# Layer two of a strided-attention and two-layer kernel: its phases in another order

## The chip, the cores and the metric

The program runs on one core of a Trainium2 chip (trn2). The time is the device time of one execution in microseconds (us); with one core there is no slowest of several. TensorE (PE) multiplies, VectorE (DVE) and ScalarE (ACT) do the elementwise work, SyncE (SP) only issues transfers. The kernel before took 868.13 us, the median of three runs (863.78 to 869.3).

## The reference

```python
def _attn_ref(q, k, v):                       # (4, 8, 576, 64), heads 0-3 local, 4-7 strided, stride 32
    scores = scale * np.matmul(q, k.transpose(0, 1, 3, 2))
    scores = np.where(masks[None], scores, -1000000000.0)
    ...                                       # softmax
    return np.matmul(attn, v).astype(np.float32)

def _moe_ref(x, w_in, w_out, s, b):           # x (2304, 512), w_in (512, 2048), w_out (2048, 512)
    r = np.maximum(x @ w_in, 0.0)
    return ((s * (r * r) + b) @ w_out).astype(np.float32)

def _moe2_ref(x, w_in, w_out):
    h = x @ w_in
    return ((h * np.cos(h)) @ w_out).astype(np.float32)
```

Attention gives `x`, layer one is `_moe_ref`, layer two `_moe2_ref`. The weights come as 64-bit floats and are turned into 32-bit ones on the chip.

## The kernel before, in words

Every 32-bit operand of a large product is split into a high half (`split_hi`, L161, a copy on ACT that rounds) and a low half (`split_lo`, L164, a subtraction on DVE), and a product is three matmuls: high by high, high by low, low by high.

The 2304 tokens are three blocks of 768. Attention and a part of layer one come first. From there on the products with `w_in` are made by seven products of half-size operands (P1 to P7) in place of eight; one unit is one pair of 128-wide slices of the 2048, eight units to a block. In this long middle part an automatic scheduler puts the instructions of each engine in order, and background jobs (`pair_ops`, `out_ops`, `sum_ops`) run a step now and a step then between the products (`bg2_step`): they load a weight, convert it, form its sums, split it and store it for later. `out_ops` does this for a slice of `w_out`; for layer two it also stores the unsplit slice (`w2f`).

The last part is `Blocks`, for blocks 1 and 2 of layer two; there each engine takes its instructions in the order in which the program writes them. It begins at unit 2 of block 1 (units 0 and 1 and block 0 come before it, and `run_out` stores the six output tiles of block 0 about there). It has two stages for each block.

*Periods.* `period(v)` makes P1 to P7 of unit v, each 6 matmuls of 128x384, in two PSUM banks that take turns from unit to unit. A bank is emptied by ACT (`evacuate`, tile `q`, L1511) or by a sum on DVE (`hsum`, L1089, 128x384), and the next product into the bank waits for that. P3 and P4 of unit v are made in period v+1. Each finished h goes through g = h cos h in five steps: `arg` (ACT, L1529), `whole` (ACT, L1533, one shared tile `m`, shown as `a`), `rest` (DVE, L1538), `sine` (ACT, L1543), `times` (DVE). The result stands in quarters `(i, f)`, shown as `graw`.

*Products with w_out.* `BLOCK_PRODUCTS` lists seven products j of four pairs each: `pair(n)`, n = 4j + pp, is 12 matmuls of 128x384 (two units, two output halves e, three terms). For its operand `hi(n)` and `lo(n)` split a quarter into one of three operand buffers, n mod 3. For some j the quarter is first replaced by a sum or a difference of quarters: `add(n)` on DVE. One 128x768 instruction does a pair of units for pp 0 and 1, two 128x384 ones for pp 2 and 3. The loop writes, for each n, `pair(n)`, then `after(j)` at the end of a phase, then `hi(n+2)`, `add(n+3)`, `lo(n+2)`. `after(0)` to `after(2)` copy two PSUM banks to tiles t0, t1, t2 on ACT; `after(3)` does four sums on DVE, `after(4)` and `after(5)` two each, and stores. For block 1, `form(2)` in the loop also takes steps that form the operands of block 2.

The two stages overlap: `run` mixes the end of the last unit's chain (unit 7, `last`) with `pair(0)`, `pair(1)` and the first splits.

Of the kernel before, what the change touches and what calls it, by code (L numbers as in the profile page):

```python
# [9 lines left out]
F32 = mybir.dt.float32  # L10
# [101 lines left out]
NSUM = 4  # L112
OPERANDS = [(0, 0), (0, 1), (3, 1)]
# [15 lines left out]
def net(ctx, tc, qkl, qks, rqk, vloc, vstr, rv, wi1, wo1, wp1, wo2, wp2, s, b, out):  # L129
# [267 lines left out]
    def out_ops(raw, ly, n):  # L397
        t = conv_tile("tw")
        yield from to_f32(t, raw)
        bg2_load()  # L400
        if ly:
            yield lambda t=t: nc.sync.dma_start(out=w2f[n // 2][:, n % 2, :], in_=t)
# [8 lines left out]
        yield lambda: None  # L411
# [1055 lines left out]
    class Blocks:  # L1467
# [15 lines left out]
        def acc(self, j, e):  # L1483
            return (accs[0:2], accs[2:4], accs[4:6], banks, accs[4:6], accs[2:4], accs[0:2])[j][e][:, :HT]
# [64 lines left out]
        def period(self, v):  # L1549
            new, old = v < NPAIR, v > self.v0  # L1550
            if new:
                self.product("P1", v)
                self.evacuate("P1", v)
            self.hsum(v - 1, 1, 1, 1, 2)
            self.whole(v - 2, 1)
            self.sine(v - 2, 0)
            if new:
                self.product("P2", v)
                self.hsum(v, 0, 0, 1, 0)
# [55 lines left out]
        def pair(self, n, units=(0, 1), es=(0, 1)):  # L1615
# [21 lines left out]

        def after(self, j):
            if j in (0, 1, 2):
# [3 lines left out]
                self.t = getattr(self, "t", []) + [t]  # L1643
# [12 lines left out]
            if j == 5:  # L1656
                o = io_p.tile([P, 2, HT], F32, tag="io", name="c21")
                for e in range(2):
                    tt(o[:, e], self.acc(j, e), self.t[0][:, e], ALU.add)
                self.store(1, 0, o)  # L1660
# [13 lines left out]

        def form(self, n):
            for _ in range(n):
                next(self.forms, None)

        def run(self):
# [330 lines left out]
```

## Time and profile before

| | us |
|---|---|
| median of three runs | 868.13 |
| lowest and highest run | 863.78, 869.3 |
| the profiled execution | 861.52 |
| its span, first to last instruction | 859.7 |
| busy in it: PE, DVE, ACT | 823.9, 680.8, 587.3 |

The profiled execution is 6.6 us below the median; rows of it are compared with its own 861.52. A row of a list of instructions gives the start in us, the duration of the group, the engine, the line of the kernel, the operation, the tiles, the count, and in square brackets the idle time of the engine just before it with what ended that. A matmul of 384 columns takes 0.33 us from start to end, but the next one starts 0.17 us after it.

### The profile page before, as it was taken

To read this page: it belongs to the slowest core of one execution; us is meant where nothing else is said; L and a number is where in the kernel's file an instruction comes from. 1 tells how busy PE (TensorE), PEld (TensorE's weight loads), DVE (VectorE), ACT (ScalarE), POOL (GpSimd) and SP (SyncE) were. 2 spreads that over 40 slices of the span, in tenths; PEclk is the share of its full clock that TensorE was granted. 3 is DMA by queue.
4 is the path that set the end of the run, shared out by engine and by line. 5 is a ranking of instruction groups with operands and counts; after the bars stand their busy time and mean duration, and the time that the engine had idled before them with its cause. 6 is when DMAs were issued, how large, how long until landed. Compare 5 with 4: busy or idle time off the path is not lost.

```text
span 859.7 us, 15559 instructions
## 1 busy us (share of the span) xinstructions
PE 823.9 (96%) x5545; PEld 734.6 (85%) x5545; DVE 680.8 (79%) x1297; ACT 587.3 (68%) x1237; POOL 19.5 (2%) x73
## 2 busy tenths in 40 slices
PE   8999999999999999999999999999998899998898
PEld 5667777888888988999989889899898789998788
DVE  6999766997897878986976987877678887578884
ACT  6888776677766867867767656656588544688443
POOL 3120000000000000000000000000000000000000
PEclk9999999999999999999999999999999999999999
DMA  9755532688779978797998989989987579772574
GB/s 339 218 176 180 158 109 96 234 290 232 260 306 317 358 279 269 277 317 220 312 359 294 318 288 340 294 324 341 365 271 234 193 230 288 239 254 89 175 240 154
DMA packets 103069, 220.00 MB, mean 256 GB/s; under 512 B 9168, under 2 KB 54480, under 8 KB 102992
## 3 DMA queue, kind: packets, MB, share of 16 engines
q1 hardware_dynamic: 101696, 212.62, 73.4%
q10 hardware_dynamic: 1296, 6.39, 2.2%
q8 instruction: 44, 0.72, 0.3%
q14 instruction: 33, 0.27, 0.1%
HBM read 163.92 MB, written 55.05 MB: 255 GB/s over the span
## 4 chain that ended last, share of the span: by engine, by line
PE 69%; DVE 9%; ACT 4%; DMA 3%; issue 1%; SPq 0%; ACTq 0%; DVEq 0%
PE acc L1775 9%; PE acc L875 9%; PE h_ps L875 8%; PE pb L1878 8%; PE pa L1878 8%; PE acc L1765 7%; PE acc L1624 6%; PE acc L1496 5%; DVE xlo L164 3%; PE pa L1496 3%; PE pb L1496 2%; DVE graw L1089 2%; ACT xhi L161 1%; PE pa L1624 1%; DVE t L1089 1%
## 5 line engine op out<-in xcount | busy, mean ns | idle before, releaser
L875 PE MATMUL h_ps<-xhi,w 128*128 128x512 f32 (+1 forms) x320 | 100.9, 377 | 0.2
L875 PE MATMUL acc<-gh,w 128*128 128x512 f32 (+1 forms) x320 | 99.1, 374 | 0.0
L1775 PE MATMUL acc<-gh,w2l 128*128 128x512 f32 (+1 forms) x384 | 85.6, 336 | 0.0
L1878 PE MATMUL pa<-xhi,wfl 128*128 128x384 f32 x268 | 80.2, 339 | 4.1 <-DVE h L1858 2.5
L1878 PE MATMUL pb<-xhi,wfl 128*128 128x384 f32 x268 | 80.1, 339 | 0.9 <-ACT q L1889 0.9
L161 ACT ACTIVATE xhi<-graw 128x384 fp32r<-128x384 f32 (+1 forms) x84 | 50.8, 629 | 43.5 <-DVE graw L1089 27.0
L1624 PE MATMUL acc<-xhi,w2m 128*128 128x384 f32 x256 | 68.1, 339 | 3.7 <-ACT xhi L161 3.7
L875 PEld LDWEIGHTS h_ps<-xhi,w 128*128 128x128 f32 x320 | 58.5, 189 | 11.7 <-ACT w L161 1.1
L164 DVE TENSOR_TENSOR xlo<-graw,xhi 128x384 fp32r<-128x384 f32 (+1 forms) x84 | 54.9, 685 | 16.4 <-ACT xhi L161 16.2
L875 PEld LDWEIGHTS acc<-gh,w 128*128 128x128 f32 x320 | 58.4, 189 | 10.1 <-ACT gh L161 0.2
L1775 PEld LDWEIGHTS acc<-gh,w2l 128*128 128x128 f32 x384 | 60.2, 188 | 7.3
L1765 PE MATMUL acc<-w2l,gh 128*128 128x512 f32 x192 | 60.2, 390 | 0.0
L1496 PE MATMUL acc<-xhi,wfl 128*128 128x384 f32 x196 | 56.1, 338 | 3.9 <-DVE graw L1089 3.6
L875 PE MATMUL h_ps<-xlo,w 128*128 128x512 f32 (+1 forms) x160 | 59.5, 372 | 0.0
L875 PE MATMUL acc<-gl,w 128*128 128x512 f32 (+1 forms) x160 | 59.3, 371 | 0.0
L1878 PEld LDWEIGHTS pa<-xhi,wfl 128*128 128x128 f32 x268 | 49.4, 188 | 7.4 <-DVE h L1858 3.6
L1878 PEld LDWEIGHTS pb<-xhi,wfl 128*128 128x128 f32 x268 | 49.4, 188 | 3.8 <-ACT q L1889 2.2
L1624 PEld LDWEIGHTS acc<-xhi,w2m 128*128 128x128 f32 x256 | 47.3, 191 | 4.0 <-ACT xhi L161 4.0
L1775 PE MATMUL acc<-gl,w2l 128*128 128x512 f32 x192 | 49.5, 336 | 0.0
L1366 ACT ACTIVATE h<-h 128x768 f32<-128x768 f32 x48 | 40.4, 841 | 12.2 <-DVE h L1858 11.9
L164 DVE TENSOR_TENSOR gl<-r,gh 128x512 fp32r<-128x512 f32 (+2 forms) x56 | 40.5, 723 | 8.9 <-ACT gh L1366 6.5
L1624 PE MATMUL acc<-xlo,w2m 128*128 128x384 f32 x128 | 43.8, 343 | 2.7 <-DVE xlo L164 2.6
(240 smaller groups left out, 2137.9 us busy)
## 6 DMA issues: line engine op xcount, KB each, us to landing
wfl<-wfb SPq DMA_DIRECT2D x68, 512.0 KB, 5.3
wfl<-wfa SPq DMA_DIRECT2D x34, 512.0 KB, 5.5
w2l<-w2s SPq DMA_DIRECT2D x28, 512.0 KB, 5.5
praw<-in_wp_dram SPq DMA_DIRECT2D x22, 512.0 KB, 4.7
oraw<-in_wo_dram SPq DMA_DIRECT2D x21, 512.0 KB, 4.4
wfb<-ob SPq DMA_DIRECT2D x21, 512.0 KB, 4.6
w2s<-ow SPq DMA_DIRECT2D x20, 512.0 KB, 5.2
w2m<-wsum SPq DMA_DIRECT2D x20, 512.0 KB, 4.3
```

Source lines behind the costliest of these rows:

```text
L161: nc.scalar.activation(dst_hi, src, AF.Copy)
L164: return nc.vector.tensor_tensor(dst_lo, src, hi.bitcast(F32), ALU.subtract)
L875: nc.tensor.matmul(*args, **kw)
L1089: return nc.vector.tensor_tensor(d, x, y, op)
L1366: return nc.scalar.activation(*args, **kw)
L1496: nc.tensor.matmul(self.bank(v, bi), a, b[:, m, :], start=st and m == 0 and i == 0, stop=m == 1 and i == 2, skip_group_check=True)
L1624: nc.tensor.matmul(self.acc(j, e), w[u][:, wi, c], g[:, u], start=first and i == 0, stop=last and i == 2, skip_group_check=True)
L1765: nc.tensor.matmul(accs[e], g[:, e * P : (e + 1) * P], w[:, wi, :], start=start and i == 0, stop=stop and i == 2, skip_group_check=True,)
L1775: nc.tensor.matmul(o, w[:, wi, e * P : (e + 1) * P], g[:, c : c + o.shape[1]], start=start and i == 0 and (c == 0 or e % 2 == 0), stop=sto ...
L1878: nc.tensor.matmul(pb[bi], a, b[:, m, :], start=st and m == 0 and i == 0, stop=m == 1 and i == 2, skip_group_check=True)
```

## The change

Six things change. (1) The order of phases: the product that uses quarter (1, 1) as it stands moves from place 5 to place 3, so that phases with an `add` (j = 1, 2, 4, 5) no longer follow one another four times; the PSUM banks follow, and the sum that makes output tile `c21` from that product comes later, in j = 5. (2) In the periods, `hi(0)` and `hi(1)` come one period earlier, `hi(2)` right behind period 7, and `lo(0)` and `lo(1)` come behind the `hsum` that opens the period. (3) Between the stages, `add(4)` to `add(7)`, `hi(4)` to `hi(6)` and the chain of unit 7 stand in another order, and `pair(0)` is cut in three. (4) The loop splits three pairs ahead, not two. (5) The sums of outputs that stood together in `after(3)` and `after(5)` are given out one at a time by the table `ROOM`, as are the steps of `form`. (6) In `out_ops` the store of the unsplit slice takes the place of an empty step, one step fewer for each of layer two's 16 slices, and the last two output tiles of block 0 take buffers of the pool `io` in place of `gt`.

```diff
     (False, 0, (1, 0), ((1, 0), (1, 0), (1, 1), "add")),
+    (False, 3, (1, 1), None),
     (False, 2, (0, 0), ((0, 0), (1, 1), (0, 0), "subtract")),
     (True, (1, 1), (0, 0), ((0, 0), (0, 1), (0, 0), "subtract")),
-    (False, 3, (1, 1), None),
     (True, (1, 0), (0, 1), None),
...
+ROOM = {9: (0, 2), 10: (0, 2), 11: (0, 2), 12: (0, 2), 20: (1, 1), 21: (1, 1), 22: (0, 2), 23: (1, 2), 24: (1, 2), 25: (0, 2), 26: (0, 2)}
...
     def out_ops(raw, ly, n):
-        t = conv_tile("tw")
+        t = whole = conv_tile("tw")
         yield from to_f32(t, raw)
         bg2_load()
-        if ly:
-            yield lambda t=t: nc.sync.dma_start(out=w2f[n // 2][:, n % 2, :], in_=t)
...
         yield lambda: split_hi(os[0], t)
-        yield lambda: None
+        yield lambda: nc.sync.dma_start(out=w2f[n // 2][:, n % 2, :], in_=whole) if ly else None
         yield lambda: split_lo(os[1], t, os[0])
...
         def acc(self, j, e):
-            return (accs[0:2], accs[2:4], accs[4:6], banks, accs[4:6], accs[2:4], accs[0:2])[j][e][:, :HT]
+            return (accs[0:2], accs[2:4], accs[4:6], accs[2:4], banks, accs[4:6], accs[0:2])[j][e][:, :HT]
...
             self.hsum(v - 1, 1, 1, 1, 2)
+            if v - 1 >= NPAIR - 3:
+                self.lo(v - 1 - NPAIR + 3)
             self.whole(v - 2, 1)
...
-                    first, last = pp == 0 and u == 0 and j < 4, pp == 3 and u == 1
+                    first, last = pp == 0 and u == 0 and j in (0, 1, 2, 4), pp == 3 and u == 1
...
+        def add_acc(self, d, j, e):
+            tt(d[:, e], self.acc(j, e), self.t[0][:, e], ALU.add)
+
         def after(self, j):
             if j in (0, 1, 2):
...
-            if j == 3:
-                u2 = self.t[0]
+            if j == 4:
                 for e in range(2):
-                    tt(u2[:, e], self.acc(j, e), u2[:, e], ALU.add)
-                tt(self.t[2], self.t[2], self.t[1], ALU.add)
-                tt(self.t[2], self.t[2], u2, ALU.add)
-                self.store(1, 1, self.t[2])
-            if j == 4:
+                    self.add_acc(self.t[0], j, e)
+            if j == 5:
                 o = io_p.tile([P, 2, HT], F32, tag="io", name="c12")
...
-            if j == 5:
-                o = io_p.tile([P, 2, HT], F32, tag="io", name="c21")
-                for e in range(2):
-                    tt(o[:, e], self.acc(j, e), self.t[0][:, e], ALU.add)
-                self.store(1, 0, o)
...
+        def c21(self):
+            self.o21 = io_p.tile([P, 2, HT], F32, tag="io", name="c21")
+            self.add_acc(self.o21, 3, 0)
+            yield
+            self.add_acc(self.o21, 3, 1)
+            self.store(1, 0, self.o21)
+            yield
+
+        def c22(self):
+            tt(self.t[2], self.t[2], self.t[1], ALU.add)
+            yield
+            tt(self.t[2], self.t[2], self.t[0], ALU.add)
+            self.store(1, 1, self.t[2])
+            yield
...
         def run(self):
             last = NPAIR - 1
...
                 self.period(v)
-                if v >= NPAIR - 2:
-                    n = v - NPAIR + 2
-                    self.hi(n)
-                    self.lo(n)
-
+                if v >= NPAIR - 3:
+                    self.hi(v - NPAIR + 3)
+
+            self.add(4)
+            self.hsum(last, 1, 1, 1, 2)
             self.pair(0, units=(0,))
-            self.hsum(last, 1, 1, 1, 2)
+            self.pair(0, units=(1,), es=(0,))
             self.sine(last - 1, 0)
             self.times(last - 1, 0)
             self.product("P3", last)
             self.hsum(last, 0, 1, 1, 1)
+            self.pair(0, units=(1,), es=(1,))
             self.whole(last - 1, 1)
             self.rest(last - 1, 1)
-            self.hi(2)
-            self.lo(2)
-            self.pair(0, units=(1,))
             self.product("P4", last)
             self.arg(last, 0)
+            self.lo(2)
             self.whole(last, 0)
             self.rest(last, 0)
+            self.pair(1)
             self.hsum(last, 1, 0, 0, 2)
-            self.pair(1)
             self.hi(3, 0)
             self.lo(3, 0)
             self.sine(last - 1, 1)
             self.sine(last, 0)
-            self.times(last - 1, 1)
             self.times(last, 0)
-            self.arg(last, 1)
+            self.hi(4)
             self.hi(3, 1)
             self.lo(3, 1)
+            self.add(5)
+            self.lo(4)
+            self.arg(last, 1)
             self.whole(last, 1)
+            self.times(last - 1, 1)
             self.rest(last, 1)
             self.sine(last, 1)
+            self.pair(2)
+            self.hi(5)
+            self.add(6)
+            self.lo(5)
+            self.pair(3)
+            self.after(0)
+            self.hi(6)
             self.times(last, 1)
-            self.add(4)
-            for n in range(2, len(BLOCK_PRODUCTS) * 4):
+            self.add(7)
+            self.lo(6)
+            for n in range(4, nb):
...
                 if pp == 3:
                     self.after(j)
-                self.hi(n + 2)
-                self.add(n + 3)
-                self.lo(n + 2)
-                if j in (0, 5, 6):
-                    self.form(2)
+                    if j == 4:
+                        self.later = self.c21()
+                    if j == 5:
+                        self.later = self.c22()
+                self.hi(n + 3)
+                self.add(n + 4)
+                self.lo(n + 3)
+                k = ROOM.get(n, (0, 0))
+                self.room(k[0])
+                self.form(k[1])
...
     def run_out(s_, e):
...
-            o = gt_p.tile([P, 512], F32, tag="gt", name="o")
+            o = io_p.tile([P, 512], F32, tag="io", name="o")
```

The first place is DVE at the end of period 7 of block 2. `acc_3814` and `acc_3816` are the same PSUM bank in the two programs, `graw` the quarters, `r_...` the argument of the cosine, `a_...` the tile `m`. Before:

```order
L1089 TENSOR_TENSOR graw<-graw,r_8652 128x768
L1538 SCALAR_TENSOR_TENSOR r_8707<-a_5686,r_8707 128x768
L164 TENSOR_TENSOR xlo<-graw,xhi 128x2x384
L1089 TENSOR_TENSOR graw<-acc_3814,q 128x384
L1089 TENSOR_TENSOR graw<-graw,r_8707 128x768
L1089 TENSOR_TENSOR graw<-acc_3814,q 128x384
```

Now:

```order
L1088 TENSOR_TENSOR graw<-graw,r_8653 128x768
L1537 SCALAR_TENSOR_TENSOR r_8708<-a_5702,r_8708 128x768
L1088 TENSOR_TENSOR graw<-graw 128x2x384
L1088 TENSOR_TENSOR graw<-acc_3816,q 128x384
L1088 TENSOR_TENSOR graw<-graw,r_8708 128x768
L1088 TENSOR_TENSOR graw<-acc_3816,q 128x384
```

The split `lo(1)` in front of the sum that empties the bank is gone from there; `add(4)`, 128x2x384 from `graw` alone, stands in its place, and it needs no result of ACT.

The second place is ACT a little later in block 2, around the last sine of unit 7. Before:

```order
L1543 ACTIVATE r_8718<-r_8718 128x768
L1543 ACTIVATE r_8766<-r_8766 128x768
L1529 ACTIVATE r_8791<-graw 128x768
L161 ACTIVATE xhi<-graw 128x384
L1533 ACTIVATE a_5686<-r_8791 128x768
L1543 ACTIVATE r_8791<-r_8791 128x768
L161 ACTIVATE xhi<-graw 128x2x384
```

Now:

```order
L1542 ACTIVATE r_8719<-r_8719 128x768
L1542 ACTIVATE r_8764<-r_8764 128x768
L162 ACTIVATE xhi<-graw 128x2x384
L162 ACTIVATE xhi<-graw 128x384
L1528 ACTIVATE r_8795<-graw 128x768
L1532 ACTIVATE a_5702<-r_8795 128x768
L1542 ACTIVATE r_8795<-r_8795 128x768
L162 ACTIVATE xhi<-graw 128x2x384
```

`r_8791` and `r_8795` are the last argument, (7, 1). The split `hi(4)`, 128x2x384, has moved from behind its sine to in front of its `arg`; behind the sine now stands `hi(5)`.

The third place is DVE at the end of the phase that uses both banks `pa` and `pb`, in block 2: j = 3 before, j = 4 now. Before:

```order
L164 TENSOR_TENSOR xlo<-graw,xhi 128x2x384
L1089 TENSOR_TENSOR t_8831<-pa,t_8831 128x384
L1089 TENSOR_TENSOR t_8831<-pb,t_8831 128x384
L1089 TENSOR_TENSOR t_8985<-t_8985,t_8908 128x768
L1089 TENSOR_TENSOR t_8985<-t_8985,t_8831 128x768
L1089 TENSOR_TENSOR graw<-graw 128x384 x2
L164 TENSOR_TENSOR xlo<-graw,xhi 128x2x384
L1089 TENSOR_TENSOR graw<-graw 128x384 x2
L164 TENSOR_TENSOR xlo<-graw,xhi 128x384 x4
L164 TENSOR_TENSOR xlo<-graw,xhi 128x2x384
```

Now:

```order
L165 TENSOR_TENSOR xlo<-graw,xhi 128x2x384
L1088 TENSOR_TENSOR t_8833<-pa,t_8833 128x384
L1088 TENSOR_TENSOR t_8833<-pb,t_8833 128x384
L1088 TENSOR_TENSOR graw<-graw 128x384 x2
L165 TENSOR_TENSOR xlo<-graw,xhi 128x384 x4
L1088 TENSOR_TENSOR c_9164<-acc_3813,t_8833 128x384
L165 TENSOR_TENSOR xlo<-graw,xhi 128x2x384
L1088 TENSOR_TENSOR c_9164<-acc_3814,t_8833 128x384
L165 TENSOR_TENSOR xlo<-graw,xhi 128x2x384
L1088 TENSOR_TENSOR c_9211<-acc_3815,t_8833 128x384
L1088 TENSOR_TENSOR c_9211<-acc_3816,t_8833 128x384
L165 TENSOR_TENSOR xlo<-graw,xhi 128x384 x2
```

The two 768-wide sums of `t_8985` (`t_8984` now) no longer stand behind the sums of `pa` and `pb`: they come one each between later splits.

## Rows read from the trace of the kernel before

**Rows 1.** The page's busy time, share and instructions of each engine.

```profile
PE 823.9 (96%) x5545; PEld 734.6 (85%) x5545; DVE 680.8 (79%) x1297; ACT 587.3 (68%) x1237; POOL 19.5 (2%) x73
```

**Rows 2.** What PE waited for, 600 to 860 us: total, times, longest.

```profile
PE acc L1624 <- ACT xhi L161: 7.3, 2, 3.7
PE acc L1624 <- DVE xlo L164: 5.5, 5, 2.1
PE acc L1496 <- DVE graw L1089: 3.6, 4, 1.7
PE pb L1496 <- DVE graw L1089: 2.4, 2, 1.7
```

**Rows 3.** Instructions of PE in order of time, block 2.

```profile
779.11 0.44 PE L1496 MATMUL pb<-xhi,wfl 128*128 128x384 f32 x1 [0.69 <-DVE graw L1089]
...
787.36 0.44 PE L1496 MATMUL acc<-xhi,wfl 128*128 128x384 f32 x1 [1.73 <-DVE graw L1089]
...
800.82 0.44 PE L1624 MATMUL acc<-xhi 128*128 128x384 f32 x1 [3.66 <-ACT xhi L161]
801.82 0.69 PE L1624 MATMUL acc<-xlo,xhi 128*128 128x384 f32 x1 [0.55 <-DVE xlo L164]
802.30 0.84 PE L1624 MATMUL acc<-xhi 128*128 128x384 f32 x2
...
804.85 0.34 PE L1624 MATMUL acc<-xlo 128*128 128x384 f32 x1
...
833.27 0.44 PE L1624 MATMUL acc<-xlo,xhi 128*128 128x384 f32 x1 [2.06 <-DVE xlo L164]
...
854.18 0.33 PE L1624 MATMUL acc<-xlo,w2m 128*128 128x384 f32 x1
...
855.91 0.34 PE L1624 MATMUL acc<-xhi,w2m 128*128 128x384 f32 x1
```

**Rows 4.** Stretches: length, busy time of engines, granted clock, DMA share, GB/s.

```profile
660.00:680.00 20.00, 15.80 (x81) 15.04 (x81) 18.12 (x27) 12.60 (x20) 0.00 (x0) 0.91 0.60 200
...
700.00:720.00 20.00, 17.95 (x104) 17.62 (x103) 17.79 (x28) 8.82 (x14) 0.00 (x0) 1.00 0.81 253
```

**Rows 5.** Instructions of DVE in order of time, block 2.

```profile
785.88 0.96 DVE L164 TENSOR_TENSOR xlo<-graw,xhi 128x768 fp32r<-128x768 f32 x1 [1.05 <-ACT xhi L161]
786.76 0.55 DVE L1089 TENSOR_TENSOR graw<-acc,q 128x384 f32<-128x384 f32 x1
...
796.14 0.96 DVE L1538 SCALAR_TENSOR_TENSOR r<-a,r 128x768 f32<-128x768 f32 x1 [0.17 <-ACT a L1533]
...
798.88 1.82 DVE L1089 TENSOR_TENSOR graw<-graw 128x768 f32<-128x768 f32 x2
...
803.48 1.02 DVE L1089 TENSOR_TENSOR graw<-graw 128x384 f32<-128x384 f32 x2
...
829.47 1.94 DVE L1089 TENSOR_TENSOR t<-t,t 128x768 f32<-128x768 f32 x2
```

**Rows 6.** Instructions of ACT in order of time, block 2.

```profile
791.41 1.57 ACT L1543 ACTIVATE r<-r 128x768 f32<-128x768 f32 x2
...
797.13 0.84 ACT L1543 ACTIVATE r<-r 128x768 f32<-128x768 f32 x1 [1.02 <-DVE r L1538]
799.92 0.84 ACT L161 ACTIVATE xhi<-graw 128x768 fp32r<-128x768 f32 x1 [1.95 <-DVE graw L1089]
```

**Rows 7.** Instructions of ACT, then of PE, in order of time, block 1.

```profile
618.19 0.49 ACT L1511 ACTIVATE q<-acc 128x384 f32<-128x384 f32 x1 [3.19 <-DMA out_dram<-o]
...
619.32 0.44 PE L1496 MATMUL acc<-xhi,wfl 128*128 128x384 f32 x1 [0.78 <-DVE graw L1089]
```

**Rows 8.** What PE waited for, 150 to 600 us: total, times, longest.

```profile
PE pa L1878 <- DVE h L1858: 2.5, 2, 1.6
PE pa L1878 <- ACT xhi L161: 1.5, 1, 1.5
PE pb L1878 <- ACT q L1889: 0.9, 1, 0.9
```

More of the change, by code (lines that the diff above doesn't have):

```diff
@@ L1549, in period @@
         def period(self, v):
[L1550 to L1553, printed above, removed]
+            old = v > self.v0
+            self.product("P1", v)
+            self.evacuate("P1", v)
             self.hsum(v - 1, 1, 1, 1, 2)
+            if v - 1 >= NPAIR - 3:
+                self.lo(v - 1 - NPAIR + 3)
             self.whole(v - 2, 1)
             self.sine(v - 2, 0)
-            if new:
-                self.product("P2", v)
-                self.hsum(v, 0, 0, 1, 0)
+            self.product("P2", v)
+            self.hsum(v, 0, 0, 1, 0)
             self.rest(v - 2, 1)
@@ L1642, in after @@
                     nc.scalar.activation(t[:, e], self.acc(j, e), AF.Copy)
-                self.t = getattr(self, "t", []) + [t]
-            if j == 3:
-                u2 = self.t[0]
+                self.t.append(t)
+            if j == 4:
                 for e in range(2):
-                    tt(u2[:, e], self.acc(j, e), u2[:, e], ALU.add)
-                tt(self.t[2], self.t[2], self.t[1], ALU.add)
-                tt(self.t[2], self.t[2], u2, ALU.add)
-                self.store(1, 1, self.t[2])
-            if j == 4:
+                    self.add_acc(self.t[0], j, e)
+            if j == 5:
                 o = io_p.tile([P, 2, HT], F32, tag="io", name="c12")
                 for e in range(2):
-                    tt(o[:, e], self.acc(j, e), self.t[0][:, e], ALU.add)
+                    self.add_acc(o, j, e)
                 self.store(0, 1, o)
-            if j == 5:
-                o = io_p.tile([P, 2, HT], F32, tag="io", name="c21")
-                for e in range(2):
-                    tt(o[:, e], self.acc(j, e), self.t[0][:, e], ALU.add)
-                self.store(1, 0, o)
             if j == 6:
@@ L1677, in form, with room @@
                 next(self.forms, None)
+        def room(self, n):
+            for _ in range(n):
+                next(self.later, None)
         def run(self):
             last = NPAIR - 1
+            nb = len(BLOCK_PRODUCTS) * 4
+            self.t = []
             for v in range(self.v0, NPAIR):
                 self.period(v)
-                if v >= NPAIR - 2:
-                    n = v - NPAIR + 2
-                    self.hi(n)
-                    self.lo(n)
+                if v >= NPAIR - 3:
+                    self.hi(v - NPAIR + 3)
+            self.add(4)
+            self.hsum(last, 1, 1, 1, 2)
             self.pair(0, units=(0,))
-            self.hsum(last, 1, 1, 1, 2)
+            self.pair(0, units=(1,), es=(0,))
             self.sine(last - 1, 0)
@@ L1708, in run @@
             self.sine(last, 0)
-            self.times(last - 1, 1)
             self.times(last, 0)
-            self.arg(last, 1)
+            self.hi(4)
             self.hi(3, 1)
             self.lo(3, 1)
+            self.add(5)
+            self.lo(4)
+            self.arg(last, 1)
             self.whole(last, 1)
+            self.times(last - 1, 1)
             self.rest(last, 1)
             self.sine(last, 1)
+            self.pair(2)
[5 more added lines that the diff above has]
+            self.hi(6)
             self.times(last, 1)
-            self.add(4)
-            for n in range(2, len(BLOCK_PRODUCTS) * 4):
+            self.add(7)
+            self.lo(6)
+            for n in range(4, nb):
                 j, pp = divmod(n, 4)
-                if n == len(BLOCK_PRODUCTS) * 4 - 1:
+                if n == nb - 1:
                     self.pair(n, es=(0,))
@@ L1727, in run @@
                     self.after(j)
-                self.hi(n + 2)
-                self.add(n + 3)
-                self.lo(n + 2)
-                if j in (0, 5, 6):
-                    self.form(2)
+                    if j == 4:
[8 more added lines that the diff above has]
+                self.form(k[1])
+            self.form(30)
     def run_out(s_, e):
```

## The prediction

> **What bounds the kernel.** I read the page's busy times first: PE is busy for 823.9 of 859.7 us and DVE, next, for 680.8 [rows 1]. No product is added or taken away, so the change can only give back time in which PE stands, and the second view is the list of what PE waited for. From 600 us on it has 18.8 us in four groups, all on DVE or ACT and none on a transfer [rows 2]; in the 450 us before, some 4.9 us [rows 8]. The third view, PE's instructions in order of time, shows where block 2 stands; block 1 repeats it, as the counts and longest waits of [rows 2] tell.
>
> A wait costs more than its idle time. From 854.18 to 855.91 ten matmuls start, one each 0.173 us, while one lasts 0.33 [rows 3]; so a stop adds the idle time and 0.16, as the last matmul's end is no longer under the next one's start. With that, a block of the last part has these stops [rows 3]:
>
> - At 779.11, in period 7: 0.69, so 0.86 us.
> - At 787.36, P3 of unit 7: 1.73, so 1.90. DVE shows why: the split at 785.88 waited 1.05 us for ACT's high half, and the sum that empties the bank stood behind it and started at 786.76 [rows 5].
> - At 800.82, `pair(4)`: 3.66, so 3.83. ACT waits 1.02 for DVE's `rest`, makes the last sine at 797.13, then waits 1.95 for `add(4)` (the first of two adds at 798.88 [rows 5]) and starts `hi(4)` at 799.92 [rows 6].
> - At 801.82: 0.55, with the slower first matmul 0.82 in all, for `lo(4)`.
> - A slow clock behind it: from 802.30 to 804.85 eight matmuls take 2.55 us where 1.38 would do (about half speed, the lower of the two levels, 1.2 GHz), and the one at 801.82 loses 0.31: 1.47 in all. In block 1 the stretch of the same stop has a granted clock of 0.91 [rows 4].
> - At 833.27: 2.06, so 2.23. The sums of `after(3)`, two of them 1.94 us at 829.47 [rows 5], stand in front of `lo(17)`.
>
> The first five make 8.88 us for each block, the last 2.23.
>
> **The sum, part by part.** Prices: on DVE a 128x768 instruction holds the queue 0.87 us (two in 1.82 [rows 5]) and is done after 0.96; one of 128x384 0.47 (two in 1.02) and 0.56. On ACT 0.73 to 0.75 (two sines in 1.57 [rows 6]) and 0.85; `arg` I take at 0.85 for both. From one engine to the other I add 0.04: 796.14 and 0.96 make 797.10, and the sine starts at 797.13 [rows 5, 6].
>
> *Periods 6 and 7.* `hi(0)` and `lo(0)` go into period 6, `hi(1)` and `lo(1)` stay in 7, each behind the opening sum. A period is 42 matmuls, 7.3 us. ACT has three copies of about 0.4 and six long steps of 0.75 to 0.85 in it, 5.8; DVE four sums of 0.47 and four long steps of 0.87, 5.4. One split more makes 6.6 and 6.2. The cover is that slack, and the split of DVE falls where it waits for P2 anyway. The stop of 0.86 goes.
>
> *The end of period 7.* I count from the copy of P7's bank, t = 0; PE begins `pair(0)` at -0.2 (its last matmul is then still running out) and is free for P3 nine matmuls later, at 1.36. DVE ends `rest` at 0.12, makes `add(4)` until 0.99, and the sum until 1.55; P3 starts at 1.59. Of 1.90 us 0.23 is left. What is late next is the last unit's chain, in which each step needs the one before: P3 is done at 2.8, its sum at 3.52 (behind `times` of unit 6), `arg` 4.40, `whole` 5.29 (it needs `m` free, so `rest(6, 1)` first), `rest` 6.29, ACT's two sines 7.21, `times` 8.21, `hi(3, 1)` 8.78, `lo(3, 1)` 9.37. PE meanwhile has the rest of `pair(0)`, P4, `pair(1)`, `pair(2)` and half of `pair(3)`, and needs that at 9.4: no stop. DVE goes on with `add(5)` (10.2), `lo(4)` (done 11.11), `times(6, 1)`, `rest(7, 1)` (12.85). `pair(4)` starts at 10.43, for `hi(4)` is long done, and its second matmul waits for `lo(4)`: 0.54. Behind `rest(7, 1)` ACT makes the sine (13.74) and only then `hi(5)` (14.5), and `lo(5)` is done at 15.5. `pair(5)` would start at 13.06: 1.48, and 0.83 more at its second matmul. Then `pair(6)` loses 0.2 for `lo(6)`. From there DVE needs 1.8 us for each pair and PE 2.08. Left are 0.23 + 0.54 + 1.48 + 0.83 + 0.2 = 3.28. No stop there is longer than those of 2.06, behind which the clock stays whole: 1.00 from 700 to 720 us, where block 1 has its own [rows 4]. So I count no slow matmuls. Gain 8.88 - 3.28 = 5.60 for each block, **11.2** in all. Bounds: the chain could hide whole (3.28 more for each block), or the stop at `pair(5)` could stay as long as today's, 3.83 + 0.82 + 1.47 = 6.12 in place of 2.31 (3.8 less). I take my own walk, whose prices all have rows.
>
> *The phases.* Behind `after(4)` DVE now has two sums (0.94), `add(23)` (0.94), `lo(22)` (0.94): done 3.0 after the bank is full, and `pair(22)` is due 4.16 after it, since the splits run three pairs ahead. The sums of c21 and c22 fall into phases without `add`, where DVE has over 1 us free in each pair. Three buffers are as many as before, so `hi(n+3)` waits for `pair(n)` where `hi(n+2)` waited for `pair(n-1)`: the same moment, only in front of other work. The steps of `form` in block 1 come twice in n = 9 to 12, at most 2.7 us of DVE to a pair for two pairs, 1.3 over, against a slack of 2.3 (two pairs of PE, 4.16, less both splits, 1.81). Gain 2 x 2.23 = **4.5**. Two of the five waits for `xlo` make 4.1 and two 1.1 of their 5.5 [rows 2]; the fifth, 0.3 in block 1, is one of the same kind and goes too: **0.5**.
>
> *Block 0's output.* ACT's copy at 618.19 waited 3.19 us for an output transfer out of a tile of pool `gt`, and PE stood 0.78 for the sum behind it [rows 7]. In `io` the tile is next wanted by an `arg` a period later. Gain **0.9**. The outputs' transfers (SP) keep their number; each store waits on SP for a sum in front of loads that PE wants six pairs, 12 us, later.
>
> *The middle.* One step fewer for each of 16 slices moves much of the scheduler's order. No row shows the new order's stops. Nearest are today's: four of 0.9 to 1.6 us, 4.9 in all, 5.6 with the 0.16 [rows 8]. They could all go, or as many come again. I take nothing, the middle of these ends.
>
> Sum: 11.2 + 4.5 + 0.5 + 0.9 = 17.1. The profiled execution would take 861.5 - 17.1 = 844.4. The median of the runs is 868.13, 6.6 above that execution; I let that stand and predict 868.1 - 17.1 = **851 us**. By itself this case reaches from 844 (the chain hides whole) to 857 (the middle doubles its stops).
>
> **A rule that speaks against it.** The row of 700 to 720 us shows one stop of 2.06 and a whole clock [rows 4]; the change leaves five shorter stops within 16 us. The Trainium skill, TensorE: Matmul & The Clock Gate, section "A second HAM failure mode: psum-queue depth-cycling", says that many short idles between groups of matmuls that cycle through PSUM banks can make the clock fall and rise again and again. No row here shows that for stops as short as these. By that rule the slow matmuls stay.
>
> **Rivals.**
>
> - *The clock falls in spite of the shorter stops.* The price is the 1.47 us of today in each block, 2.9: 854. For it: the five stops lie close, and two of them, 1.48 and 0.83, have one matmul between. Against: behind the single stop of 2.06 it did not fall [rows 4].
> - *The chain stays.* If ACT or DVE get to `hi(5)` as late as now to `hi(4)`, 3.8 come back in each block: 859. For it: `hi(5)` stands behind the last sine just as `hi(4)` did. Against: the three instructions behind that sine today (`times`, two adds) now stand elsewhere.
> - *The middle gives it back.* A stop there costs up to 1.6 + 0.16 [rows 8]; seven more of them make 12, and 863.
> - *Slower.* One mechanism: in `out_ops` the step that went lay between a job's conversion and the split that needs the output tile of the job before the last, whose store must have landed. If ACT stands there in the queue, in front of the copies that empty PE's banks, in each of the 16 jobs, at 1.78 each, that is 28.5: 851 + 28.5 = 880. It decides from 15 of the 16 jobs on (17.1 + 8.7 for 1%). Against: the scheduler can put other work there, and today's stops in the middle are four [rows 8].
> - *It doesn't do what it says.* PE's stops shrink, but PE then meets weights that are late, as the same loads are wanted 17 us earlier; none of the waits of [rows 2] is for one, and the DMA share there is 0.60 [rows 4]. 862 to 868.
>
> **Chances.** Forecast 0.56, clock 0.12, chain stays 0.14, middle gives back 0.08, slower 0.04, late weights 0.06. A measurement tells 1%, 8.7 us, from no change, so faster means below 859.4: forecast and clock, over half of the chain's case and a third of the middle's, 0.79. Slower 0.04, the rest 0.17. The range is 845 to 860: the forecast's own but for its ends, the clock's and the chain's.
>
> **What would show it.** Right: no stop of PE over 2.5 us after 620 us; none in period 7; P3 of unit 7 within 0.5 us; two stops at `pair(5)` with the last sine ahead of `hi(5)` on ACT; a granted clock of 1.00 in both stretches that had 0.91; no stop at the end of the phase with banks `pa` and `pb`; the copy of P7 in unit 2 without a transfer in front. Wrong: a stop of 3 us or more between the stages, or more than 10 us of waits from 300 to 600 us, or PE waiting for a load.

## The result, and the profile after

The changed kernel takes 843.0 us (median of four runs, 840.19 to 843.75), the kernel before, beside it, 867.07 (four runs); the ratio is 0.972, with an interval of 0.968 to 0.976. It is faster, as forecast, but 8 us below the forecast of 851 and 2 us below the range. The profiled execution took 840.19 us, its span 838.4. To read these numbers: executions of the same kernel lie 1% apart and differ in their mean granted clock, so medians are compared with medians and traces with traces.

The page's busy times after: PE stands for 19.7 us of the span, against 35.8 before [rows 1].

```profile
PE 818.7 (98%) x5545; PEld 732.4 (87%) x5545; DVE 679.5 (81%) x1297; ACT 586.8 (70%) x1237; POOL 19.8 (2%) x73
```

What PE waited for from 600 to 860 us (total, times, longest), and below it from 150 to 600 us:

```profile
PE acc L1623 <- ACT xhi L162: 2.3, 2, 1.2
PE acc L1623 <- DVE xlo L165: 1.6, 4, 0.5
PE pa L1495 <- DMA wfl<-wfb: 0.2, 1, 0.2
```

```profile
PE pa L1909 <- ACT q L1920: 1.2, 1, 1.2
PE pa L1909 <- DVE graw L1088: 1.1, 2, 0.7
PE acc L1806 <- DVE part L1088: 0.8, 1, 0.8
PE pb L1909 <- ACT q L1920: 0.7, 1, 0.7
PE pa L1909 <- DVE h L1889: 0.2, 1, 0.2
```

Of 18.8 us in the last part [rows 2] 4.1 are left. The view of before has a fifth group, which [rows 2] and the prediction leave out (19.2 with it); it is gone too:

```profile
PE acc L1496 <- DVE o L1741: 0.4, 1, 0.4
```

The stops at the sums that empty banks are gone. A stop of 0.2 for a weight is new; a wait for a load was one of the prediction's signs of being wrong, but at this size it decides nothing. The middle has 4.0 in place of 4.9 [rows 8], at other places.

PE's instructions in order of time, block 2, P3 of unit 7 to `pair(5)`; then DVE and ACT in the same stretch:

```profile
772.93 0.44 PE L1495 MATMUL acc<-xhi,wfl 128*128 128x384 f32 x1
...
782.47 0.44 PE L1623 MATMUL acc<-xlo,xhi 128*128 128x384 f32 x1 [0.24 <-DVE xlo L165]
...
785.82 0.44 PE L1623 MATMUL acc<-xhi 128*128 128x384 f32 x1 [1.16 <-ACT xhi L162]
786.81 0.44 PE L1623 MATMUL acc<-xlo,xhi 128*128 128x384 f32 x1 [0.55 <-DVE xlo L165]
```

```profile
781.47 0.95 DVE L165 TENSOR_TENSOR xlo<-graw,xhi 128x768 fp32r<-128x768 f32 x1
782.34 0.95 DVE L1088 TENSOR_TENSOR graw<-graw,r 128x768 f32<-128x768 f32 x1
783.21 0.95 DVE L1537 SCALAR_TENSOR_TENSOR r<-a,r 128x768 f32<-128x768 f32 x1
...
785.80 0.96 DVE L165 TENSOR_TENSOR xlo<-graw,xhi 128x768 fp32r<-128x768 f32 x1 [0.71 <-ACT xhi L162]
```

```profile
771.33 0.49 ACT L1510 ACTIVATE q<-acc 128x384 f32<-128x384 f32 x1
...
784.19 0.84 ACT L1542 ACTIVATE r<-r 128x768 f32<-128x768 f32 x1 [2.49 <-DVE r L1537]
784.94 0.83 ACT L162 ACTIVATE xhi<-graw 128x768 fp32r<-128x768 f32 x1
```

These are the places of [rows 3, 5, 6]. Counted from the copy at 771.33, P3 starts at 1.60 (1.59 in my walk) and the last sine at 12.86 (12.89); `lo(4)` is the instruction of DVE at 781.47, and `hi(5)` stands behind the sine. In period 7 and at the end of the phase with `pa` and `pb` there is no stop. From the first matmul of the periods to the last of all, block 1's unit 2 on, it is 225.7 us where it was 246.3; the prediction's terms for this stretch made 17.1. The clock of the two stretches of [rows 4]:

```profile
660.00:680.00 20.00, 18.07 (x100) 16.93 (x99) 18.46 (x29) 12.04 (x21) 0.00 (x0) 1.00 0.69 234
700.00:720.00 20.00, 20.00 (x117) 19.77 (x115) 15.76 (x25) 9.46 (x16) 0.00 (x0) 1.00 0.95 306
```

So the mechanism of the forecast stands in the trace nearly as it was walked. The question for the experiments is where 8 us more came from.

### The profile page after: what moved, and what is told of

Same layout as the page of the kernel before. It is cut to its first block, busy times and chain, and to the rows that moved or that the text cites. A ratio compares the mean times of both kernels' runs of the same rounds, so it can differ in the third digit from the quotient of the medians.

```text
span 838.4 us, 15528 instructions
## 1 busy us (share of the span) xinstructions
PE 818.7 (98%) x5545; PEld 732.4 (87%) x5545; DVE 679.5 (81%) x1297; ACT 586.8 (70%) x1237; POOL 19.8 (2%) x73
## 4 chain that ended last, share of the span: by engine, by line
PE 77%; DVE 4%; DMA 3%; ACT 2%; issue 1%; SPq 0%; DVEq 0%; ACTq 0%
PE acc L1806 10%; PE acc L1623 10%; PE acc L874 9%; PE pa L1909 9%; PE pb L1909 8%; PE h_ps L874 8%; PE acc L1796 8%; PE acc L1495 6%; PE pa L1495 3%; PE pb L1495 2%; DVE graw L1088 1%; PE pa L1623 1%; PE pb L1623 1%; DMA wsum<-xhi 1%; DVE xlo L165 1%; DMA praw<-in_wp_dram 1%
## 5 line engine op out<-in xcount | busy, mean ns | idle before, releaser
L162 ACT ACTIVATE xhi<-graw 128x384 fp32r<-128x384 f32 (+1 forms) x84 | 51.1, 630 | 35.8 <-PE acc L1623 16.1
L1909 PE MATMUL pa<-xlo,wfl 128*128 128x384 f32 x134 | 45.0, 336 | 0.0
```

The source lines that it names most:

```text
L162: nc.scalar.activation(dst_hi, src, AF.Copy)
L1909: nc.tensor.matmul(pb[bi], a, b[:, m, :], start=st and m == 0 and i == 0, stop=m == 1 and i == 2, skip_group_check=True)
```

## The experiments

The first four run together on one chip, beside 24 runs of the kernel before (median 865.41). Each does one part of the change alone.

**1. The seam alone.** Periods, seam and splits three pairs ahead as changed; phases, `after`, `out_ops` and `run_out` as before; the steps of `form` come from j = 4 on.

```diff
-                self.hi(n + 2)
-                self.add(n + 3)
-                self.lo(n + 2)
-                if j in (0, 5, 6):
+                self.hi(n + 3)
+                self.add(n + 4)
+                self.lo(n + 3)
+                if j in (4, 5, 6):
                     self.form(2)
```

> The kernel before with the new order of the periods and of the seam between the stages alone, splits three pairs ahead; phases, output sums, out_ops and buffers as before. Theory A (the gain is the sum of PE's stops in the last part, and my walk of the seam is right): the stops at P3 of unit 7, at pair(4) and the slow matmuls go, 2.8 to 3.3 us a block are left, and the profiled execution is 11 to 14 us below that of the kernel before (848 to 851); the two stops of about 2 us at the end of phase j = 3 stay. Theory B (the executions of the kernel before lie above the profiled one because the long stop and its slow matmuls vary from execution to execution): the median falls by more than that, 14 to 18 us, to 850 to 853, as near to its own profiled execution as in the changed kernel (about 3 us). Rival to B (the distance has to do with something else): the median falls by the same 11 to 14 us, to 854 to 857, and stays 5 to 7 us above the profiled execution.

Measured: 849.21 us (848.98 to 850.97), ratio 0.981 (0.976 to 0.985), 16.2 us by the medians; the profiled execution took 848.98. What PE waited for in it from 600 to 870 us:

```profile
PE acc L1624 <- DVE xlo L164: 2.9, 6, 0.8
PE acc L1624 <- ACT xhi L161: 2.3, 2, 1.2
PE acc L1496 <- DVE graw L1089: 1.1, 2, 0.8
PE pa L1496 <- DMA wfl<-wfb: 0.5, 1, 0.5
PE acc L1496 <- DVE o L1754: 0.4, 1, 0.4
```

The seam's stops are those of the changed kernel. But the expectation that the 2.06 us stops stay is wrong: with the third pair of lead block 2 has none, and block 1 has two of 0.55 and 0.77 in their place. Part of what I booked under the phases is the lead's. The profiled execution is 12.5 us below that of before, the median 16.2 below, as theory B has it. But a profiled execution of before that was merely a fast one would look the same, and its 861.52 lies below all 24 runs beside this one.

**2. The phases alone.** `BLOCK_PRODUCTS`, the banks, `after`, `c21`, `c22` and `ROOM` as changed; two pairs of lead and the seam as before.

```diff
+                    if j == 4:
+                        self.later = self.c21()
+                    if j == 5:
+                        self.later = self.c22()
                 self.hi(n + 2)
                 self.add(n + 3)
                 self.lo(n + 2)
+                k = ROOM.get(n, (0, 0))
+                self.room(k[0])
+                self.form(k[1])
```

> The kernel before with the new order of the phases and the output sums given out one at a time alone; seam, splits two pairs ahead, out_ops and buffers as before. Theory A: the stop of 2.06 us at the end of the phase with banks pa and pb goes in both blocks, 4.5 to 5.5 us; the stops of the seam stay, the 3.66 us one with its slow matmuls too. Time 862 to 864. Theory B adds nothing here, since the long stop stays. Rival (the spread only pays with splits three pairs ahead): a stop of 0.5 to 1 us per block is left at that place, 864 to 866.

Measured: 863.85 us (860.90 to 866.74), ratio 0.998 (0.996 to 1.000): 1.6 us. Its waits for `xlo`, 600 to 870 us, are half of the 5.5 in the kernel before [rows 2]:

```profile
PE acc L1625 <- DVE xlo L165: 2.8, 8, 0.7
```

By its time it is within theory A, by its stops nearer the rival. Two of the eight, 0.39 and 0.30, stand behind the long stop of the seam as before. In the phases block 2 has one of 0.20 left in place of 2.06, block 1 five of 0.20 to 0.70, 1.9 in all. Why the median gains less than these waits shrank is not shown.

**3. `out_ops` alone**, one step shorter.

```diff
-        if ly:
-            yield lambda t=t: nc.sync.dma_start(out=w2f[n // 2][:, n % 2, :], in_=t)
...
-        yield lambda: None
+        yield lambda: nc.sync.dma_start(out=w2f[n // 2][:, n % 2, :], in_=whole) if ly else None
```

> The kernel before with out_ops one step shorter alone (the store in place of the empty step). My prediction's term: no change, 867 to 869. What the two traces say (the middle 1.2 us shorter, the first part 0.5 longer): 866.5 to 867.5. Rival (the distance between the median and the profiled execution comes from the middle's transfers, which the shorter job moves): 863 to 865.

Measured: 861.55 us (860.01 to 865.02), ratio 0.995 (0.992 to 0.997): 3.9 us, beyond the rival's 863 to 865. My term for it was 0.

**4. The two output tiles in `io` alone.**

```diff
-            o = gt_p.tile([P, 512], F32, tag="gt", name="o")
+            o = io_p.tile([P, 512], F32, tag="io", name="o")
```

> The kernel before with the last two output tiles of block 0 in buffers of pool io alone. My prediction's term: ACT's copy of P7 in unit 2 no longer waits for a transfer, PE's stop of 0.78 goes, 0.9 us in all: 867.2. If the small stops around it (three matmuls between 611 and 615 us that start 0.15 to 0.52 late) have the same cause, up to 2.2 us: 866. Rival (the transfer itself is what is late, and another copy waits for it): no change.

Measured: 864.38 us (863.23 to 872.54), ratio 1.000 (0.997 to 1.003): no difference that can be told. PE in its profiled execution:

```profile
615.58 0.44 PE L1496 MATMUL acc<-xhi,wfl 128*128 128x384 f32 x1 [1.13 <-ACT q L1511]
...
623.73 0.41 PE L1496 MATMUL pa<-xhi,wfl 128*128 128x384 f32 x1 [0.97 <-DMA wfl<-wfb]
```

The stop of 0.78 behind the late copy [rows 7] is gone, but the time is lost beside it. The stop of 1.13 has taken the place of the 0.4 for `o`: ACT's copy stands behind a split that waited 1.66 us for a store to land:

```profile
611.88 0.63 ACT L161 ACTIVATE xhi<-t 128x512 fp32r<-128x512 f32 x1 [1.66 <-DMA wsum<-xhi]
```

And a weight is late, 0.97. In the nine traces with these tiles in `io` it is late in seven (0.24 to 1.17), in the six without in two (0.47 and 0.32 in 1 and 2).

This execution took 867.71 us, 6.2 more than the one that I had read, and shows where such a difference sits. Windows of it (columns as in [rows 4]) and PE behind the stop at the end of j = 3 in block 1:

```profile
660.00:680.00 20.00, 15.00 (x69) 14.09 (x70) 17.55 (x26) 13.28 (x22) 0.00 (x0) 0.86 0.50 169
700.00:720.00 20.00, 17.94 (x95) 17.62 (x94) 15.70 (x26) 7.47 (x12) 0.00 (x0) 0.91 0.70 224
```

```profile
708.23 0.44 PE L1624 MATMUL acc<-xlo,w2m 128*128 128x384 f32 x1 [2.06 <-DVE xlo L164]
708.51 0.75 PE L1624 MATMUL acc<-xhi,w2m 128*128 128x384 f32 x2
...
711.94 0.38 PE L1624 MATMUL acc<-xlo,w2m 128*128 128x384 f32 x1
712.15 0.51 PE L1624 MATMUL acc<-xhi,w2m 128*128 128x384 f32 x2
```

From the matmul at 708.51 to the one at 712.15 twelve start in 3.64 us, 2.08 at full pace: 1.56 lost at the lower level, behind the very stop whose whole clock was my evidence [rows 4]. The stretch at 660 is longer too.

The second group ran on one chip beside 15 runs of before (865.58).

**5. The long stop filled.** The kernel before, with matmuls whose results nobody uses ahead of `pair(4)`.

```diff
+                if n == 4:
+                    for i in range(20):
+                        nc.tensor.matmul(self.acc(1, i % 2), wt[0][:, 0, 0:P], gt[:, 0], start=True, stop=True, ...)
```

> The kernel before with 20 extra matmuls (results unused, same shape, into the two banks that pair(4) overwrites) in the stop of 3.66 us ahead of pair(4), in both blocks; nothing else. Theory B (the length of the slow stretch behind that stop varies from execution to execution, 1.5 to 3.2 us a block so far, and sets the distance of the median from the profiled execution): pair(4) starts when it did, but no matmul behind it is slow; the median falls by 3 to 6 us, to 859.5 to 862.5, and the spread of the runs shrinks. Rival (the slow stretch is the cost of something else at pair(4), its weights or the split): the slow matmuls stay, no change, or up to 1 us slower where the extra matmuls run over.

Measured: 864.64 us (861.23 to 865.21), ratio 0.998 (0.996 to 1.000), 0.9 us. The matmuls behind the filled stop are whole in both blocks, so the slow stretch does come from the stop. But both stops of 2.06 us have a slow stretch in this execution, and `pair(5)` of block 1 waits 0.3 for its low half, a stop that the trace of before, with its slow matmuls, does not have. The gain is below what theory B gave.

**6. The changed kernel with the old `out_ops`.** The diff is that of 3, reversed.

> The changed kernel with the out_ops of the kernel before (one step more); all else as changed. Theory C (the scheduler's old order has a stop of PE between 430 and 445 us, where ACT stands behind the landing of a store of its output tile, 0.9 to 2.05 us in four traces, and the new order has not): that stop is back, and the median is 2 to 4 us above the changed kernel's. Rival (my prediction: the middle is worth nothing, and the 3.9 us of the out_ops change alone came from less slow clock behind it): within 1 us of the changed kernel.

Measured: 847.28 us (845.12 to 849.48) against 843.29 for the changed kernel (8): 4.0 us, as theory C has it. ACT and PE at the place:

```profile
436.56 0.63 ACT L162 ACTIVATE ow<-tw 128x512 fp32r<-128x512 f32 x1 [1.20 <-DMA wfb<-ob]
437.10 0.83 ACT L1367 ACTIVATE h<-h 128x768 f32<-128x768 f32 x1
437.83 0.47 ACT L1922 ACTIVATE q<-pb 128x384 f32<-128x384 f32 x1
```

```profile
438.36 0.45 PE L1911 MATMUL pb<-xhi,wfl 128*128 128x384 f32 x1 [1.21 <-ACT q L1922]
```

The split `ow` of an `out_ops` job waits for a store to land, and ACT's copy that empties `pb` stands behind it. In the seven traces with the old `out_ops` this stop of PE is 0.9 to 2.1 us, in each within 0.02 of ACT's wait for the store, and in the one I read before predicting 0.9, the shortest. In the eight with the new one there is none from 430 to 445. But the new order has a stop of its own behind a store, near 331, 0.9 to 2.1 us in all eight; here in the changed kernel's first profile, DVE, ACT and PE:

```profile
328.68 0.56 DVE L1115 TENSOR_TENSOR xt<-xhi,xt 128x384 f32<-128x384 f32 x1 [2.10 <-DMA w2f<-tw]
329.74 0.67 ACT L170 ACTIVATE tw<-oraw 128x512 f32<-128x512 f32 x1 [1.86 <-DVE xlo L165]
330.83 0.44 PE L1909 MATMUL pa<-xhi,wfl 128*128 128x384 f32 x1 [1.18 <-ACT q L1920]
```

DVE waits there for the store that the change moved. So the change trades stops. The stops over 0.1 us of the whole middle, from its first matmul to the first of the periods, make 5.0 to 8.1 us in the seven, on average 6.5, and 3.6 to 5.3 in the eight, on average 4.3. The middle itself takes 341.6 to 346.6 us in the seven, on average 344.1, and 340.1 to 344.2 in the eight, on average 341.3: the traces show 2.8 of the 4 us. The execution that I read had the shortest of the seven. The clock is not what differs: the runs' mean is 0.992 in 3 and 0.993 in before, and 0.997 in both 6 and 8.

**7. One more order of the seam, spoiled.** In this kernel `hi(5)` is written ahead of `pair(2)`, and as the two share a buffer `pair(2)` multiplies the operand of `pair(5)`.

```diff
+            self.hi(5)
+            self.lo(5)
...
             self.pair(2)
-            self.hi(5)
...
-            self.lo(5)
```

> The changed kernel with the seam in one more order: add(5), lo(3,1) and lo(4) at once behind hi(3,1), then hi(5), lo(5), add(6), and only then the tail of unit 7's f = 1 chain (times of unit 6, rest, sine and times of unit 7, given out behind pairs 4, 5 and 6). If my walk of the seam is right (PE stands at pair(4) and pair(5) because lo(4) is behind the chain on DVE and hi(5) behind the last sine on ACT): the stops of 0.24, 1.15 and 0.55 us with 0.16 to 0.3 each go, about 2.5 us a block, 4 to 5 us in all. Rival (the chain then comes late for add(11), or DVE is full there): the stops move to pairs 6 to 9, gain under 2 us.

Measured: 848.70 us. PE waited 3.43 us, in both blocks, for that wrong operand:

```profile
788.02 0.69 PE L1623 MATMUL acc<-xhi,w2m 128*128 128x384 f32 x1 [3.43 <-ACT xhi L162]
```

It tells nothing of the question asked, and one thing beside: behind these stops too the clock fell, in both blocks.

**8. The changed kernel again.**

> The changed kernel once more, on the chip of the other three, so that they can be compared. Theory B: a narrow spread, 840 to 844, the profiled execution within 3 us of the median, and no slow stretch behind any stop of the last part. Rival (the clock falls there in some executions as it does in the kernel before): runs of 846 and more at a granted clock of 0.99 or less.

Measured: 843.29 us (841.47 to 844.94), the runs' granted clock 0.995 to 0.998. The spread is nearly as expected, but there is a slow stretch, in block 1:

```profile
660.00:680.00 20.00, 18.07 (x92) 17.17 (x92) 18.21 (x29) 11.74 (x21) 0.00 (x0) 0.91 0.62 219
```

```profile
667.57 0.45 PE L1623 MATMUL acc<-xhi,w2m 128*128 128x384 f32 x1 [1.14 <-ACT xhi L162]
668.57 0.44 PE L1623 MATMUL acc<-xlo,w2m 128*128 128x384 f32 x1 [0.55 <-DVE xlo L165]
...
669.19 0.46 PE L1623 MATMUL acc<-xlo,w2m 128*128 128x384 f32 x1
...
672.84 0.33 PE L1623 MATMUL acc<-xlo,w2m 128*128 128x384 f32 x1
```

From 669.19 to 672.84 twelve matmuls start in 3.65 us, 1.57 lost, behind stops of 1.14 and 0.55, which kept the clock whole in the first trace.

The third group ran beside 17 runs of before (865.53), the last two kernels beside 11 (865.91).

**9. The seam in one more order, with the buffers in turn.**

```diff
             self.hi(4)
             self.hi(3, 1)
+            self.add(5)
             self.lo(3, 1)
-            self.add(5)
             self.lo(4)
-            self.arg(last, 1)
-            self.whole(last, 1)
-            self.times(last - 1, 1)
-            self.rest(last, 1)
-            self.sine(last, 1)
             self.pair(2)
             self.hi(5)
-            self.add(6)
             self.lo(5)
+            self.add(6)
+            self.arg(last, 1)
+            self.whole(last, 1)
             self.pair(3)
-            self.after(0)
             self.hi(6)
-            self.times(last, 1)
             self.add(7)
+            self.after(0)
             self.lo(6)
...
+                if n == 4:
+                    self.times(last - 1, 1)
+                if n == 5:
+                    self.rest(last, 1)
+                    self.sine(last, 1)
+                if n == 6:
+                    self.times(last, 1)
```

> The changed kernel with the seam in one more order, where the operand buffers keep their turn: add(5) ahead of lo(3,1) and lo(4); hi(5), lo(5), add(6), hi(6), add(7) behind them; and the tail of the f = 1 chain (times of unit 6, rest, sine and times of unit 7), which add(11) is the first to need, given out behind pairs 4, 5 and 6. If my walk of the seam is right (PE stands at pair(4) and pair(5) because DVE has the chain in front of lo(4), and ACT the last sine in front of hi(5)): of the stops of 0.24, 1.16 and 0.55 us none over 0.3 is left at pairs 4 to 6, one of about 0.6 appears at pair(10), 1.9 us less a block, and with shorter stops no slow stretch: 838 to 840 against 843. Rival (DVE is the bound of the whole stretch to add(11), so that every us saved at pair(5) comes back behind it): gain under 1 us.

Measured: 837.09 us (834.70 to 839.97), ratio 0.967 (0.965 to 0.970), the granted clock 1.000 in four of six runs. What PE waited for, 600 to 860 us:

```profile
PE acc L1623 <- DVE xlo L165: 1.1, 2, 0.6
PE pa L1495 <- DMA wfl<-wfb: 0.5, 1, 0.5
```

The stops at pairs 4 to 6 are gone, and one of 0.55, 0.82 from start to start, appears at `pair(10)`. So the walk's reasons for what was left are right. The gain over kernel 8, 6.2 us, is more than the 3.8 that I expected from the stops; the slow stretches went with them.

**10. The sums of outputs not spread.** In `ROOM`, 19 and 23 get both sums.

```diff
-ROOM = {..., 20: (1, 1), 21: (1, 1), 22: (0, 2), 23: (1, 2), 24: (1, 2), ...}
+ROOM = {..., 19: (2, 0), 20: (0, 1), 21: (0, 1), 22: (0, 2), 23: (2, 2), 24: (0, 2), ...}
```

> The changed kernel with the sums of c21 and c22 not spread: both sums of c21 behind pair(19), both of c22 behind pair(23), as they stood together before; the order of phases and splits three pairs ahead as changed. If the spread gave the gain of the phases: a stop of 1 to 2 us a block is back at pair(21) or pair(25), 2 to 4 us in all, 845 to 847. Rival (the third pair of lead covers sums of 1.9 us by itself, as block 2 of the seam-only kernel has no stop there): no stop, 842 to 844.

Measured: 846.69 us (844.51 to 847.54), within the first expectation, but not for its reason: no stop waits for DVE at these pairs. There is one of 0.7 for a weight, and both blocks have a slow stretch behind the seam's stops; the runs' clock is 0.993 to 0.994.

**11. Both long stops filled**: 5, and 11 matmuls more ahead of `pair(17)`.

> The kernel before with extra matmuls (results unused) in both long stops of each block: 20 in the 3.66 us ahead of pair(4) as before, and 11 in the 2.06 us of pair(17), into banks that are free. Theory B (the clock falls behind long stops in a part of the executions, and that is some 2 us of the distance between median and profiled execution): mean granted clock of the runs 0.998 or more against 0.993, and the median 3 to 4 us lower, 861.5 to 863. Rival (the fills only shift the slow stretches to other places, or the time is lost elsewhere): clock 0.996 as with one fill, and a gain under 2 us.

Measured: 863.71 us (861.27 to 866.89), ratio 0.998 (0.996 to 1.000), 1.8 us. The runs' clock is 0.998 on average (0.993 for before), and the windows of all four places show 1.00; the filled stop:

```profile
803.74 3.63 PE L1724 MATMUL acc<-xhi 128*128 128x384 f32 x20
807.58 0.44 PE L1624 MATMUL acc<-xhi 128*128 128x384 f32 x1 [0.20 <-ACT xhi L161]
```

Theory B's mechanism holds, its size does not: filling is worth about 2 us of the kernel before, not 3 to 4, and that is the rival's figure. The profiled execution, 866.89, the slowest of the twelve, still has a slow stretch, in the middle, behind a stop of 2.12 at 336.

**12 and 13. Kernel 9 with lumped sums, and kernel 9 again.**

> The kernel of the seam in one more order, with the sums of c21 and c22 not spread (both of c21 behind pair(19), both of c22 behind pair(23)). The run before with lumped sums was slower without a stop at those sums, but at a lower granted clock behind the stops of the seam; here those stops are gone. If the spread is worth something by itself: 2 to 4 us above the next kernel, with a stop at pair(21), (22), (25) or (26). If the third pair of lead covers the lumped sums, and the 3 us were slow matmuls: within 1 us of the next kernel, clock 0.998 or more in both.

> The kernel of the seam in one more order once more, on the chip of the run above: 836 to 838, clock 0.998 to 1.000, no slow stretch in the last part. If its six runs had only met no slow stretch by chance: runs of 839 to 841 at a clock of 0.996 or less.

Measured: 837.51 us (836.66 to 837.84) and 836.20 (835.82 to 838.17), ratio 0.966 (0.963 to 0.969) for the second; clock 1.000 in five of six runs of each. So most of the 3.4 us of kernel 10 was slow matmuls. The 1.3 that remain are near the spread, but the trace names a stop that makes 0.9 of it. PE of kernel 12, and what its SP issued:

```profile
712.24 0.45 PE L1623 MATMUL acc<-xlo,xhi 128*128 128x384 f32 x1 [0.72 <-DMA w2m<-w2s]
```

```profile
707.21 2.60 SPq L1268 DMA_DIRECT2D w2m<-w2s  x3
710.04 0.41 SPq L1635 DMA_DIRECT2D out_dram<-t  x1
710.50 0.52 SPq L1268 DMA_DIRECT2D w2m<-w2s  x1
```

SPq is SP issuing transfers. The store of output tile c22 stands there in front of a weight's load; in kernel 13 it is issued at 711.70, behind the four loads that end before 709.4. Kernel 10 has the same stop of 0.72, no kernel with spread sums has it, and neither 10 nor 12 has a stop for DVE at these sums. So what spreading changes is seen in SP's queue, not in DVE's. That it makes the 1.3 us is not shown: the last part takes 223.4 us in the trace of 12 and 223.5 in that of 13, which loses 0.9 more to the weight at 617.

## Why the prediction missed by 8 us

| | forecast | shown |
|---|---|---|
| seam and phases | 11.2 + 4.5 + 0.5 = 16.2 | 16.2 (1) + 1.6 (2) = 17.8 |
| the middle | 0 | 3.9 (3), 4.0 (6) |
| block 0's output | 0.9 | none that can be told (4) |
| starting point | 868.13 | 865.6, the median of 67 more runs |

The gains of seam and phases are taken from medians and hold what the clock gave with them: 0.996 in 1 against 0.993 in before. Starting point and middle make 6.5 us of the 8, seam and phases 1.6. The parts shown add up to 21.7, and 22.3 lie between 865.6 and the 843.3 of kernel 8.

- **The middle was the step that failed.** I put it at nothing, "the middle of these ends", from four stops in one trace; the shorter `out_ops` is worth 3.9 and 4.0 us. One of the four is an `out_ops` job that waits for a store, with ACT's copies behind it: the mechanism that I priced as the rival "slower" was in the kernel before. The new order does not have that stop but has one of its own behind a store, and fewer us of stops in all, 4.3 in place of 6.5 on average. I read the trace with the least, 5.0. The traces show 2.8 of the 4 us; where the rest lies stays open.
- **The starting point.** I kept the 6.6 us between the profiled execution and the median. Four of them are real: the execution of 861.52 was faster than each of 67 later runs (862.46 to 872.18). By experiment 11 some 2 us of that is the clock, and 2.5 the middle (341.6 against 344.1 on average, experiment 6); both are smaller in the changed kernel, whose profile lies 2.8 below its median. The other 2.5 was the median of only three runs, luck and no mechanism.
- **The seam was right in its walk.** What was left, 3.28 us a block in the sum, measures 2.9 in block 2 (0.24, 0.41, 1.33, 0.82 and 0.09, from start to start). Short losses that are no stop in the list were not counted: four matmuls in the phases that start 0.2 late, some 1.4 us of late starts at 611 to 614, and 0.11 on the second matmul behind each stop.
- **The phases were right in sum.** The walk used the third pair of lead and the new order together. Either alone does most of it: the lead leaves no stop in block 2 and 1.3 us in block 1 (1), the order 0.2 and 1.9 (2); with both none is left, and the sums need not be spread for it (10).
- **The clock.** "No slow matmuls" held in the profiled execution and not in general. Behind stops of 3.4 to 3.7 us the clock fell in 10 of 10 cases of all traces, behind 2.06 in 3 of 8, behind the pair of 1.14 and 0.55 in 4 of 10, in the seam of kernels 9, 12 and 13, with stops up to 0.55, in none of 6. So my single row was too little to go by: in those 4 of 10 the slow matmuls stay, in the other six they do not, and that the first trace of the changed kernel has none was in part luck. The Trainium skill (TensorE: Matmul & The Clock Gate, "A second HAM failure mode: psum-queue depth-cycling"), which tells of frequent short idles that make the clock swing, is borne out by the four and not by the six; in no trace did it fall twice behind one stop.
- **Block 0's output** went as walked on ACT, but PE's time is lost beside it, to a weight or to ACT's copy behind a split (4). Late weights were a rival, priced by rows of one trace in which none is late; 1 and 2, with the old tiles, show that they can be late there without this change.

## What to carry to other kernels

A stop that ends on a transfer has a length of its own in each execution: read such a stop in more than one trace before its price, or its absence, goes into a sum. When a chain delays operands, ask which consumer is the first to need its end and give its tail out behind later work: kernel 9 took 6 us more in this way. An elementwise sum moved in a queue also moves its store, so follow SP's order to the loads behind it.

## What was not expected of the hardware

Whether the clock falls behind a stop of 1.1 to 2.1 us differs from execution to execution of one kernel; each slow stretch in the last part lost 1.5 to 2.8 us here. In the middle it fell in four traces, behind stops of 0.97 (7), 1.88 (1), 1.91 (5) and 2.12 (11). Over 67 runs of the kernel before, a mean granted clock lower by 0.001 goes with 0.7 us more.
